# Spreading softmax probabilities as 32-bit words, a changed load order and program order, in a one-core decode block

## The chip, the cores and the metric

The kernel runs on one core of a Trainium2 chip. The metric is the time of one execution in device microseconds (us). In a trace, time counts from the start of the core's span; the span of the kernel before was 86.6 us where its time was 88.59, so some 2 us lie outside it. PE is the matrix engine (PEld its weight loads), DVE the vector engine, ACT the scalar engine, POOL is GpSimd, and SP issues the loads. PSUM is the memory that PE's results stand in, and a load lands when its data has arrived. In the views, `[1.76 <-issue]` means that the engine idled 1.76 us before this line and that the profile shows nothing that it waited for; another name after the arrow is what it waited for. The granted clock is a share of PE's full clock. L123 is a line of the kernel, with numbers of its own in each version.

## The reference

One decode step of a block with conditioned layer norms: four sequences, one new token each, width 512, 32 query heads on 8 key/value heads of 128, the last 1024 of 4096 cached positions, a feed-forward layer of 1792.

```python
mod = (silu(c) @ w_mod).reshape(4, 6, 1, 512)            # sa, ca, ga, sb, cb, gb
h = layernorm(x) * (1 + ca) + sa
q = (h @ wq) ...                                         # 32 heads x 128
scores = q @ k[:, :, -1024:].T * Dh ** -0.5              # per sequence and head
o = softmax(scores) @ v[:, :, -1024:]
x = x + ga * (o @ wo)
h = layernorm(x) * (1 + cb) + sb
x = x + gb * (relu(h @ w1) @ w2)
```

The arithmetic is small. What is large is what has to be read: K and V windows, w_mod, wq, wo, w1 and w2, about 32 MB.

## The kernel before

All large loads go through one queue, in this order: w_mod, three K tiles, wq, five K tiles, eight V tiles, wo in four quarters, w1, and w2 in three pieces. A tile of K or V is 1 MB. The 11 buffers for K and V and the shared buffers of w_mod with w1/w2 and of wq with wo make late loads wait for early readers; the trace shows 1.7 us of that, in four pieces, all of them V loads waiting for K tiles to be transposed.

```python
    KAHEAD = 3
    ...
    nc.sync.dma_start(out=wmod_sb[:], in_=w_mod...)
    for gi in range(KAHEAD): load_k(gi)
    for t in range(DT): nc.sync.dma_start(out=wq_sb[:, t, :], in_=wq_src[:, t, :])
    for gi in range(KAHEAD, NG): load_k(gi)
    ...                                                   # V, wo, w1
    W2_CHUNKS = [(0, 3), (3, 6), (6, FT2)]
    for (m0, m1) in W2_CHUNKS:
        nc.sync.dma_start(out=w2_dst[:, m0:m1, :], in_=w2_src[:, m0:m1, :])
```

The scores of all heads and sequences stand in one 128 x 1024 PSUM tile. For P times V (P: the probabilities) they have to be transposed, and each row must be spread over four column slots, of which only that of its own sequence may be nonzero. The kernel does this per quarter of the columns, with a 0/1 mask `m4`. Three slots are written by DVE, the fourth by GpSimd:

```python
    for iq in range(NQ):                                  # four quarters of 256
        nc.scalar.activation(out=e_sb[:, ws], in_=sc_ps[:, ws], func=ACT.Exp, ...)   # fp32
        for b in range(B):
            eng = nc.gpsimd if b == B - 1 else nc.vector
            eng.tensor_scalar_mul(out=p_rep[:, ws, b], in0=e_sb[:, ws], scalar1=m4[:, b:b + 1])
        ...                                               # 8 transposes into PSUM, copy to pT
```

The order of the instructions on each engine is chosen by the framework's scheduler. After P times V (`oT_ps`) come the output projection (`y_ps`, fed by wo), the second layer norm, and the feed-forward products (`u_ps` with w1, `z_ps` with w2).

Of the kernel before, what the change touches and what calls it, by code (L numbers as in the profile page):

```python
# [8 lines left out]
ACT = mybir.ActivationFunctionType  # L9
ALU = mybir.AluOpType  # L10
AX = mybir.AxisListType
bf16 = mybir.dt.bfloat16
f32 = mybir.dt.float32


@with_exitstack
def kernel(
# [14 lines left out]
    nc = tc.nc  # L32
    P = 128
# [19 lines left out]
    RB = KC  # L53
    KAHEAD = 3

    const = ctx.enter_context(tc.tile_pool(name="const", bufs=1))
    wts = ctx.enter_context(tc.tile_pool(name="wts", bufs=1))
    kvpool = ctx.enter_context(tc.tile_pool(name="kvpool", bufs=11))
    ktp = ctx.enter_context(tc.tile_pool(name="ktp", bufs=KAHEAD + 1))
    work = ctx.enter_context(tc.tile_pool(name="work", bufs=1))  # L60
# [7 lines left out]

    wmod_sb = wts.tile([P, DT, 6 * D], bf16, tag="med", name="wmod_sb")
    nc.sync.dma_start(out=wmod_sb[:], in_=w_mod.rearrange("(t p) n -> p t n", p=P))  # L70

# [3 lines left out]
    def load_k(gi):  # L75
        b, par = gi // 2, gi % 2
        kt_ = kvpool.tile([P, NI, Dh], bf16, tag="kv", name=f"k{gi}")
        nc.sync.dma_start(
            out=kt_[:].rearrange("p j d -> p (j d)"),
            in_=k_src[b, par, :, S - W:, :].rearrange("h (p j) d -> p h (j d)", j=NI),  # L80
        )
        k_tiles.append(kt_)

    for gi in range(KAHEAD):
        load_k(gi)
    wq_sb = wts.tile([P, DT, Hq * Dh], bf16, tag="big", name="wq_sb")
    wq_src = A_wq.rearrange("(t p) n -> p t n", p=P)
# [31 lines left out]
    for (m0, m1) in W2_CHUNKS:  # L119
# [4 lines left out]
    ident_bf = const.tile([P, P], bf16, name="ident_bf")  # L124
    make_identity(nc, ident_bf[:])
    ident_f = const.tile([P, P], f32, name="ident_f")
    make_identity(nc, ident_f[:])
# [5 lines left out]
    nc.gpsimd.memset(eps_t[:], EPS)  # L133
    siluT32 = const.tile([P, DT, CG], bf16, name="siluT32")
    nc.gpsimd.memset(siluT32[:], 0.0)

    ident_k = const.tile([P, P], bf16, name="ident_k")
    nc.vector.tensor_copy(out=ident_k[:].rearrange("p (h k) -> p h k", h=NHW),
                          in_=ident_bf[:].rearrange("p (k h) -> p h k", h=NHW))

    sel_l = const.tile([P, NL, P // NL], bf16, name="sel_l")
    nc.vector.tensor_copy(out=sel_l[:], in_=ident_bf[:].rearrange("p (k l) -> p l k", l=NL))

    m4 = const.tile([P, B], f32, name="m4")
    nc.vector.tensor_reduce(out=m4[:], in_=ident_f[:].rearrange("p (hp b r) -> p b hp r", b=B, r=rep),
                            axis=AX.XY, op=ALU.add)
    qpad = const.tile([P, B, 2, NHW, CG], bf16, name="qpad")
    nc.gpsimd.memset(qpad[:], 0.0)
    uT32 = const.tile([P, FT, CG], bf16, name="uT32")
    nc.gpsimd.memset(uT32[:], 0.0)  # L150
    NH = 2
    DH2 = D // NH
    xs2 = const.tile([P, DT, CG], f32, name="xs2")
# [18 lines left out]
    xT = work.tile([P, DT, B], f32, name="xT")  # L172
    nc.vector.tensor_copy(out=xT[:], in_=tp0[:, :, B:2 * B])


# [49 lines left out]

    sc_ps = psS.tile([P, W], f32, tag="s", name="sc_ps")
    IQ = NI // 4

    def k_transposes(gi):
        kT = ktp.tile([P, NI, NHW, KC], bf16, tag="kT", name=f"kT{gi}")  # L230
        for iq in range(4):
            tp = psA.tile([P, IQ, P], bf16, tag="t", name=f"ktp_{gi}_{iq}")
            for ii in range(IQ):
                nc.tensor.transpose(out=tp[:, ii, :], in_=k_tiles[gi][:, iq * IQ + ii, :], identity=ident_k[:])  # L234
            dst = kT[:, iq * IQ:(iq + 1) * IQ].rearrange("p i h k -> p i (h k)")
            if iq % 2 == 0:
                nc.vector.tensor_copy(out=dst, in_=tp[:])  # L237
            else:
                nc.scalar.copy(out=dst, in_=tp[:])  # L239
        return kT  # L240

    def k_scores(gi, kT):
        b, par = gi // 2, gi % 2
        for half in range(2):
            for hw in range(NHW):
                nc.tensor.matmul(  # L246
                    out=sc_ps[hw * CG:(hw + 1) * CG, half * HALF:(half + 1) * HALF],
                    lhsT=qpad[:, b, par, hw, :],
                    rhs=kT[:, half * (NI // 2):(half + 1) * (NI // 2), hw, :],
                    start=(gi == 0), stop=(gi == NG - 1),  # L250
                    tile_position=(0, hw * CG),
                )

    kts_pending = [k_transposes(gi) for gi in range(KAHEAD)]


    qT_ps = psA.tile([P, 2, NHW, rep, B], f32, tag="t", name="qT_ps")
    qT_v = qT_ps[:].rearrange("p a h r b -> p (a h r) b")
    for t in range(DT):
        for hq in range(Hq):  # L260
            nc.tensor.matmul(out=qT_v[:, hq, :], lhsT=wq_sb[:, t, hq * Dh:(hq + 1) * Dh], rhs=hT[:, t, :],  # L261
                             start=(t == 0 and hq == 0), stop=(t == DT - 1 and hq == Hq - 1))
    for gi in range(NG):
        b, par = gi // 2, gi % 2
        c0 = 16 * par + 4 * b
        src = qT_ps[:, par, :, :, b]
        if gi % 2 == 0:
            nc.vector.tensor_copy(out=qpad[:, b, par, :, c0:c0 + rep], in_=src)
        else:
            nc.scalar.copy(out=qpad[:, b, par, :, c0:c0 + rep], in_=src)  # L270

    for gi in range(KAHEAD - 1):
        k_scores(gi, kts_pending.pop(0))
    for gi in range(KAHEAD - 1, NG):
        if gi + 1 < NG:
            kts_pending.append(k_transposes(gi + 1))
        k_scores(gi, kts_pending.pop(0))


# [6 lines left out]
    IQ = NI // NQ  # L286
    e_sb = work.tile([P, W], f32, name="e_sb")
    den4 = work.tile([P, NQ], f32, name="den4")
    p_rep = ktp.tile([P, W, B], bf16, tag="kT", name="p_rep")
    pT = ktp.tile([P, NI, P], bf16, tag="kT", name="pT")  # L290
# [3 lines left out]
    def pv(h, i0, i1, first=False, last=False):  # L294
        par, hw = h // NHW, h % NHW
        c0 = 32 * hw + 16 * par
        for i in range(i0, i1):
            nc.tensor.matmul(out=oT_ps[:, hw, par].rearrange("p b r -> p (b r)"), lhsT=v_tiles[h][:, i, :],  # L298
                             rhs=pT[:, i, c0:c0 + B * rep], start=(first and i == i0), stop=(last and i == i1 - 1))

    VEARLY = 3
    for iq in range(NQ):
        ws = slice(iq * WQ, (iq + 1) * WQ)
        nc.scalar.activation(out=e_sb[:, ws], in_=sc_ps[:, ws], func=ACT.Exp, bias=nb[:], scale=scale,  # L304
                             accum_out=den4[:, iq:iq + 1])
        for b in range(B):
            eng = nc.gpsimd if b == B - 1 else nc.vector
            eng.tensor_scalar_mul(out=p_rep[:, ws, b], in0=e_sb[:, ws], scalar1=m4[:, b:b + 1])  # L308
        tp = psA.tile([P, IQ, P], bf16, tag="t", name=f"pT_ps{iq}")
        for ii in range(IQ):  # L310
            i = iq * IQ + ii
            nc.tensor.transpose(out=tp[:, ii, :], in_=p_rep[:, i * KC:(i + 1) * KC, :].rearrange("q k b -> q (k b)"),  # L312
                                identity=ident_bf[:])
        if iq % 2 == 0:
            nc.scalar.copy(out=pT[:, iq * IQ:(iq + 1) * IQ, :], in_=tp[:])  # L315
        else:
            nc.vector.tensor_copy(out=pT[:, iq * IQ:(iq + 1) * IQ, :], in_=tp[:])
# [9 lines left out]
    for iq in range(NQ):  # L327
        for h in range(VEARLY):
            pv(h, iq * IQ, (iq + 1) * IQ, first=(iq == 0 and h == 0))
    rb_ps = psA.tile([P, P], f32, tag="t", name="rb_ps")  # L330
    nc.tensor.matmul(out=rb_ps[:], lhsT=ones_f[:], rhs=rdiag[:], start=True, stop=True)
    rb = work.tile([P, P], f32, name="rb")
    nc.scalar.copy(out=rb[:], in_=rb_ps[:])
    for h in range(VEARLY, Hkv):
        pv(h, 0, NI, last=(h == Hkv - 1))
    oT_sb = work.tile([P, NHW, 2, B, rep], bf16, name="oT_sb")
    nc.vector.tensor_tensor(out=oT_sb[:].rearrange("p h a b r -> p (h a b r)"),
# [3 lines left out]
    for l in range(NL):  # L341
        for r in range(rep):
            nc.tensor.matmul(out=o4_ps[r * RB:(r + 1) * RB, l], lhsT=sel_l[:, l, :], rhs=oT_sb[:, :, :, :, r],
                             start=True, stop=True, tile_position=(0, r * RB))
# [20 lines left out]
    for t in range(DT):  # L365
        nh, tl = t // 2, t % 2
        nc.tensor.matmul(out=x12_ps[nh * CG:(nh + 1) * CG, tl * P:(tl + 1) * P], lhsT=xs2[:, t, :], rhs=ident_f[:],
                         start=True, stop=True, tile_position=(0, nh * CG))

    w1_cols = [w1_sb[:, t, :].rearrange("p (m2 q e) -> p m2 e q", q=P, e=2) for t in range(DT)]  # L370
# [60 lines left out]
```

## Time and profile before

| | before |
|---|---|
| time, median | 88.61 us (88.54 to 88.84, 3 runs) |
| span of the traced run | 86.6 us |
| read from HBM | 31.99 MB |
| PE / DVE / ACT / POOL busy | 63 / 32 / 27 / 11 % |

The slices, the chain of waits, the landings and the windows of the end are in the prediction below. Two more views belong to the argument. The groups of instructions that write the spread probabilities (busy us, mean ns of one, then idle time before them and what ended it):

```profile
L308 POOL TENSOR_SCALAR p_rep<-e_sb,m 128x256 bf16<-128x256 f32 x4 | 6.9, 1846 | 46.3 <-ACT e_sb L304 46.3
L312 PE MATMUL pT_ps<-ident_bf,p_rep 128*128 128x128 bf16 x32 | 4.1, 310 | 7.0 <-POOL p_rep L308 5.8
...
L308 DVE TENSOR_SCALAR p_rep<-e_sb,m 128x256 bf16<-128x256 f32 x12 | 4.4, 536 | 0.7 <-ACT e_sb L304 0.7
```

PE waits 5.8 us here for GpSimd's multiplies. And the timeline of PE near the end (start, length, instruction, idle before it):

```profile
68.99 0.41 PE L353 MATMUL y_ps<-o,wo_sb 128*128 128x4 bf16 x10 [0.40 <-DVE o L346]
71.16 3.29 PE L353 MATMUL y_ps<-o,wo_sb 128*128 128x4 bf16 x118 [1.76 <-issue]
...
80.13 3.17 PE L385 MATMUL z_ps<-w,uT 128*32 128x256 bf16 x28
```

### The profile page before, as it was taken

The numbers are of one execution on the slowest core, as the hardware profiler recorded it, in microseconds if no ns is written. First come the engines' busy times: TensorE is split into PE (matmuls) and PEld (weight loads), VectorE is DVE, ScalarE is ACT, GpSimd is POOL, SyncE is SP. The second block draws the span as 40 slices with busy tenths as digits, with TensorE's granted clock in tenths as the row PEclk, the third lists the DMA queues.
The fourth block names the chain that finished last, engine by engine and source line by source line (L and its number), as shares of the span: only waits on it lengthen the run. The fifth ranks groups of instructions, "written<-read, shape, count | busy, mean of one in ns | idle before, by whom it ended". The sixth has DMA issues, their size and how long they took to land.

```text
span 86.6 us, 2393 instructions
## 1 busy us (share of the span) xinstructions
PE 54.6 (63%) x1074; PEld 46.0 (53%) x1074; DVE 27.9 (32%) x74; ACT 23.4 (27%) x39; POOL 9.9 (11%) x19
## 2 busy tenths in 40 slices
PE   0000089799974389999997003959939619677940
PEld 0000086799974335778873003649939619557710
DVE  3704003373810030665453693283000200233130
ACT  2301001246950030877777260440100000020000
POOL 7600000000000000000000099920000000000000
PEclk9999999999998555999999985555555555555555
DMA  3799999999999999999999999999999999998100
GB/s 39 289 425 431 435 420 424 416 420 424 420 424 408 416 424 420 412 424 424 424 420 412 420 416 424 424 416 412 410 401 408 410 399 403 400 386 309 47 0 2
DMA packets 6009, 32.14 MB, mean 371 GB/s; under 512 B 480, under 2 KB 496, under 8 KB 3440
## 3 DMA queue, kind: packets, MB, share of 16 engines
q1 hardware_dynamic: 5976, 31.99, 91.0%
q8 instruction: 8, 0.13, 0.6%
q10 hardware_dynamic: 24, 0.01, 0.1%
q14 instruction: 1, 0.01, 0.0%
HBM read 31.99 MB, written 0.00 MB: 369 GB/s over the span
## 4 chain that ended last, share of the span: by engine, by line
PE 39%; DMA 33%; DVE 8%; issue 6%; ACT 5%; POOL 4%; POOLq 1%; DVEq 0%; ACTq 0%
DMA wq_sb<-in_A_wq_dram 21%; DMA wmod_sb<-in_w_mod_dram 12%; PE ktp L234 9%; PE oT_ps L298 8%; PE sc_ps L246 6%; PE y_ps L353 4%; POOL p_rep L308 4%; PE z_ps L385 4%; ACT kT L239 3%; PE pT_ps L312 2%; PE u_ps L378 2%; DVE p_rep L308 1%; DVE mx L281 1%; POOLq L426 1%; PE qT_ps L261 1%
## 5 line engine op out<-in xcount | busy, mean ns | idle before, releaser
L234 PEld LDWEIGHTS <-k 128*128 128x128 bf16 x256 | 17.0, 109 | 1.7 <-issue 1.7
L234 PE MATMUL ktp<-ident_k,k 128*128 128x128 bf16 x256 | 17.8, 238 | 0.0
L239 ACT COPY kT<-ktp 128x1024 bf16<-128x1024 bf16 x16 | 15.4, 1018 | 7.3 <-PE ktp L234 6.6
L237 DVE COPY kT<-ktp 128x1024 bf16<-128x1024 bf16 x16 | 11.1, 691 | 10.3 <-PE ktp L234 10.1
L308 POOL TENSOR_SCALAR p_rep<-e_sb,m 128x256 bf16<-128x256 f32 x4 | 6.9, 1846 | 46.3 <-ACT e_sb L304 46.3
L312 PE MATMUL pT_ps<-ident_bf,p_rep 128*128 128x128 bf16 x32 | 4.1, 310 | 7.0 <-POOL p_rep L308 5.8
L298 PE MATMUL oT_ps<-pT,v 128*128 128x16 bf16 x256 | 7.4, 175 | 1.4 <-issue 1.4
L298 PEld LDWEIGHTS <-v 128*128 128x128 bf16 x256 | 7.4, 105 | 1.6 <-issue 1.5
L312 PEld LDWEIGHTS <-p_rep 128*128 128x128 bf16 x32 | 3.1, 140 | 8.1 <-POOL p_rep L308 8.1
L246 PE MATMUL sc_ps<-kT,qpad 128*32 128x512 bf16 x64 | 6.5, 478 | 1.1 <-ACT kT L239 0.7
L261 PE MATMUL qT_ps<-hT,wq_sb 128*128 128x4 bf16 x128 | 3.9, 166 | 3.1 <-DMA wq_sb<-in_A_wq_dram 3.0
L261 PEld LDWEIGHTS <-wq_sb 128*128 128x128 bf16 x128 | 3.6, 99 | 3.4 <-DMA wq_sb<-in_A_wq_dram 3.4
L181 PE MATMUL mT<-siluT,wmod_sb 128*128 128x4 bf16 x80 | 2.3, 167 | 4.5 <-DMA wmod_sb<-in_w_mod_dram 4.5
L214 ACT ACTIVATE lnv_ln<-var_ln,eps_t 128x4 f32<-128x4 f32 x2 | 0.6, 298 | 16.7 <-DVE var_ln L212 16.7
L353 PE MATMUL y_ps<-o,wo_sb 128*128 128x4 bf16 x128 | 3.7, 166 | 2.2 <-issue 1.8
L353 PEld LDWEIGHTS <-wo_sb 128*128 128x128 bf16 x128 | 3.6, 104 | 2.2 <-issue 2.2
L181 PEld LDWEIGHTS <-wmod_sb 128*128 128x128 bf16 x80 | 2.2, 104 | 4.6 <-DMA wmod_sb<-in_w_mod_dram 4.6
L308 DVE TENSOR_SCALAR p_rep<-e_sb,m 128x256 bf16<-128x256 f32 x12 | 4.4, 536 | 0.7 <-ACT e_sb L304 0.7
L159 PE MATMUL tp<-ident_bf,cx_sb 8*128 8x8 bf16 x4 | 0.2, 163 | 6.4 <-DMA cx_sb<-in_A_x_dram 6.4
L246 PEld LDWEIGHTS <-qpad 128*32 128x32 bf16 x64 | 2.0, 109 | 3.8 <-issue 2.4
L159 PEld LDWEIGHTS <-cx_sb 8*128 8x128 bf16 x4 | 0.2, 100 | 6.4 <-issue 6.4
L315 ACT COPY pT<-pT_ps 128x1024 bf16<-128x1024 bf16 x2 | 2.0, 1012 | 4.6 <-PE pT_ps L312 4.6
(77 smaller groups left out, 42.7 us busy)
## 6 DMA issues: line engine op xcount, KB each, us to landing
k<-in_A_k_cache_dram SPq DMA_DIRECT2D x8, 1024.0 KB, 19.9
v<-in_A_v_cache_dram SPq DMA_DIRECT2D x8, 1024.0 KB, 20.2
wq_sb<-in_A_wq_dram SPq DMA_DIRECT2D x4, 1024.0 KB, 18.6
wo_sb<-in_A_wo_dram SPq DMA_DIRECT2D x4, 1024.0 KB, 20.1
wmod_sb<-in_w_mod_dram SPq DMA_DIRECT2D x1, 3072.0 KB, 10.4
w<-in_B_w_dram SPq DMA_DIRECT2D x1, 1792.0 KB, 22.2
w<-in_B_w_dram SPq DMA_DIRECT2D x2, 768.0 KB, 18.1
w<-in_B_w_dram SPq DMA_DIRECT2D x1, 256.0 KB, 13.7
```

What stands on the lines that cost most here:

```text
L181: nc.tensor.matmul(out=mT[:, k, m, :], lhsT=wmod_sb[:, t, n0:n0 + P], rhs=siluT32[:, t, 0:B], start=(t == 0), stop=(t == DT - 1))
L234: nc.tensor.transpose(out=tp[:, ii, :], in_=k_tiles[gi][:, iq * IQ + ii, :], identity=ident_k[:])
L237: nc.vector.tensor_copy(out=dst, in_=tp[:])
L239: nc.scalar.copy(out=dst, in_=tp[:])
L246: nc.tensor.matmul(out=sc_ps[hw * CG:(hw + 1) * CG, half * HALF:(half + 1) * HALF], lhsT=qpad[:, b, par, hw, :], rhs=kT[:, half * (NI // 2 ...
L261: nc.tensor.matmul(out=qT_v[:, hq, :], lhsT=wq_sb[:, t, hq * Dh:(hq + 1) * Dh], rhs=hT[:, t, :], start=(t == 0 and hq == 0), stop=(t == DT ...
L298: nc.tensor.matmul(out=oT_ps[:, hw, par].rearrange("p b r -> p (b r)"), lhsT=v_tiles[h][:, i, :], rhs=pT[:, i, c0:c0 + B * rep], start=(fi ...
L308: eng.tensor_scalar_mul(out=p_rep[:, ws, b], in0=e_sb[:, ws], scalar1=m4[:, b:b + 1])
L312: nc.tensor.transpose(out=tp[:, ii, :], in_=p_rep[:, i * KC:(i + 1) * KC, :].rearrange("q k b -> q (k b)"), identity=ident_bf[:])
L315: nc.scalar.copy(out=pT[:, iq * IQ:(iq + 1) * IQ, :], in_=tp[:])
L353: nc.tensor.matmul(out=y_ps[:, m, :], lhsT=wo_sb[:, h, l, m * P:(m + 1) * P], rhs=o4[:, l, h % NHW, h // NHW, :], start=(h == 0 and l == 0 ...
L385: nc.tensor.matmul(out=z_ps[nh * CG:(nh + 1) * CG, :], lhsT=uT32[:, m, :], rhs=w2_sb[:, m, nh * DH2:(nh + 1) * DH2], start=(m == 0), stop= ...
```

## The change

It takes GpSimd out of the softmax: exponentials are stored as bf16 in an order that puts two chunks' values into one 32-bit word, and DVE spreads such words with an AND against an all-ones or zero mask, four instructions in place of sixteen. It loads two K tiles before w_mod in place of three after it, and it runs PE, ACT, DVE and POOL in the order of the program text, with the softmax loop taken apart to suit. Some smaller things go with it: two copies of q in place of eight, a later broadcast of the denominator's reciprocal, constants in another order.

```diff
-    KAHEAD = 3
+    KAHEAD = 2
+    ctx.enter_context(tc.manual_schedule(engines={PE, Activation, DVE, Pool}))     # shortened
 ...
-    nc.sync.dma_start(out=wmod_sb[:], in_=w_mod...)
     for gi in range(KAHEAD):
         load_k(gi)
+    nc.sync.dma_start(out=wmod_sb[:], in_=w_mod...)
 ...
+    kts_pending = [k_transposes(gi) for gi in range(KAHEAD)]                       # now ahead of w_mod's matmuls
+    nc.vector.tensor_scalar_mul(out=mi4[:], in0=m4[:], scalar1=-1.0)               # int32: 0 or all ones
 ...
-    e_sb = work.tile([P, W], f32, name="e_sb")
+    e_sb = work.tile([P, W], bf16, name="e_sb")
+    e_w = e_sb[:].bitcast(i32)
-    p_rep = ktp.tile([P, W, B], bf16, tag="kT", name="p_rep")
+    p_rep = ktp.tile([P, NI // 2, P, 2], bf16, tag="kT", name="p_rep")
+    p_w = ...                                                                      # p_rep as 32-bit words
 ...
     for iq in range(NQ):
-        nc.scalar.activation(out=e_sb[:, ws], in_=sc_ps[:, ws], func=ACT.Exp, ...)
-        for b in range(B):
-            eng = nc.gpsimd if b == B - 1 else nc.vector
-            eng.tensor_scalar_mul(out=p_rep[:, ws, b], in0=e_sb[:, ws], scalar1=m4[:, b:b + 1])
+        nc.scalar.activation(out=e_sb[:, ws]..."q u k e", in_=sc_ps[:, ws]..."q u k e", func=ACT.Exp, ...)
+    for iq in range(NQ):
+        nc.vector.tensor_tensor(out=p_w[:, ws, :], in0=e_w[:, ws]..., in1=mi4[:]..., op=ALU.bitwise_and)
+    for iq in range(NQ):
         ...
-            nc.tensor.transpose(..., in_=p_rep[:, i * KC:(i + 1) * KC, :]...)
+            nc.tensor.transpose(..., in_=p_rep[:, i // 2, :, i % 2], ...)
```

More of the change, by code (lines that the diff above doesn't have):

```diff
@@ L13 @@
 f32 = mybir.dt.float32
+i32 = mybir.dt.int32
 @with_exitstack
@@ L53 @@
     RB = KC
-    KAHEAD = 3
+    KAHEAD = 2
+    NH = 2
+    DH2 = D // NH
+    ctx.enter_context(tc.manual_schedule(engines={
+        mybir.EngineType.PE, mybir.EngineType.Activation, mybir.EngineType.DVE, mybir.EngineType.Pool}))
     const = ctx.enter_context(tc.tile_pool(name="const", bufs=1))
@@ L58 @@
     kvpool = ctx.enter_context(tc.tile_pool(name="kvpool", bufs=11))
-    ktp = ctx.enter_context(tc.tile_pool(name="ktp", bufs=KAHEAD + 1))
+    ktp = ctx.enter_context(tc.tile_pool(name="ktp", bufs=4))
     work = ctx.enter_context(tc.tile_pool(name="work", bufs=1))
@@ L67 @@
     nc.scalar.dma_start(out=cx_sb[B:2 * B, :], in_=A_x.rearrange("b o d -> (b o) d"))
-    wmod_sb = wts.tile([P, DT, 6 * D], bf16, tag="med", name="wmod_sb")
-    nc.sync.dma_start(out=wmod_sb[:], in_=w_mod.rearrange("(t p) n -> p t n", p=P))
     k_src = A_k_cache.rearrange("b (par hw) s d -> b par hw s d", par=2)
@@ L85 @@
         load_k(gi)
+    wmod_sb = wts.tile([P, DT, 6 * D], bf16, tag="med", name="wmod_sb")
+    nc.sync.dma_start(out=wmod_sb[:], in_=w_mod.rearrange("(t p) n -> p t n", p=P))
     wq_sb = wts.tile([P, DT, Hq * Dh], bf16, tag="big", name="wq_sb")
@@ L125 @@
     make_identity(nc, ident_bf[:])
+    ident_k3 = const.tile([P, NHW, KC], bf16, name="ident_k")
+    nc.gpsimd.memset(ident_k3[:], 0.0)
+    nc.gpsimd.affine_select(out=ident_k3[:], in_=ident_k3[:], compare_op=ALU.not_equal, fill=1.0, base=0,
+                            pattern=[[-1, NHW], [-NHW, KC]], channel_multiplier=1)
+    ident_k = ident_k3[:].rearrange("p h k -> p (h k)")
+    siluT32 = const.tile([P, DT, CG], bf16, name="siluT32")
+    nc.gpsimd.memset(siluT32[:], 0.0)
     ident_f = const.tile([P, P], f32, name="ident_f")
@@ L133 @@
     nc.gpsimd.memset(eps_t[:], EPS)
-    siluT32 = const.tile([P, DT, CG], bf16, name="siluT32")
-    nc.gpsimd.memset(siluT32[:], 0.0)
-    ident_k = const.tile([P, P], bf16, name="ident_k")
-    nc.vector.tensor_copy(out=ident_k[:].rearrange("p (h k) -> p h k", h=NHW),
-                          in_=ident_bf[:].rearrange("p (k h) -> p h k", h=NHW))
-    sel_l = const.tile([P, NL, P // NL], bf16, name="sel_l")
-    nc.vector.tensor_copy(out=sel_l[:], in_=ident_bf[:].rearrange("p (k l) -> p l k", l=NL))
-    m4 = const.tile([P, B], f32, name="m4")
-    nc.vector.tensor_reduce(out=m4[:], in_=ident_f[:].rearrange("p (hp b r) -> p b hp r", b=B, r=rep),
-                            axis=AX.XY, op=ALU.add)
-    qpad = const.tile([P, B, 2, NHW, CG], bf16, name="qpad")
-    nc.gpsimd.memset(qpad[:], 0.0)
+    QB = 2 * NHW * CG
+    QS = QB + rep
+    qpad_f = const.tile([P, B * QS], bf16, name="qpad")
+    nc.gpsimd.memset(qpad_f[:], 0.0)
+    qpad = qpad_f[:, 0:B * QB].rearrange("p (b a h c) -> p b a h c", b=B, a=2, h=NHW)
+    qpad_s = qpad_f[:].rearrange("p (b x) -> p b x", b=B)
     uT32 = const.tile([P, FT, CG], bf16, name="uT32")
     nc.gpsimd.memset(uT32[:], 0.0)
-    NH = 2
-    DH2 = D // NH
     xs2 = const.tile([P, DT, CG], f32, name="xs2")
@@ L173, with k_transposes, k_scores @@
     nc.vector.tensor_copy(out=xT[:], in_=tp0[:, :, B:2 * B])
+    sc_ps = psS.tile([P, W], f32, tag="s", name="sc_ps")
+    IQ = NI // 4
+    def k_transposes(gi):
+        kT = ktp.tile([P, NI, NHW, KC], bf16, tag="kT", name=f"kT{gi}")
+        for iq in range(4):
+            tp = psA.tile([P, IQ, P], bf16, tag="t", name=f"ktp_{gi}_{iq}")
+            for ii in range(IQ):
+                nc.tensor.transpose(out=tp[:, ii, :], in_=k_tiles[gi][:, iq * IQ + ii, :], identity=ident_k)
+            dst = kT[:, iq * IQ:(iq + 1) * IQ].rearrange("p i h k -> p i (h k)")
+            if iq % 2 == 1:
+                nc.vector.tensor_copy(out=dst, in_=tp[:])
+            else:
+                nc.scalar.copy(out=dst, in_=tp[:])
+        return kT
+    def k_scores(gi, kT):
+        b, par = gi // 2, gi % 2
+        for half in range(2):
+            for hw in range(NHW):
+                nc.tensor.matmul(
+                    out=sc_ps[hw * CG:(hw + 1) * CG, half * HALF:(half + 1) * HALF],
+                    lhsT=qpad[:, b, par, hw, :],
+                    rhs=kT[:, half * (NI // 2):(half + 1) * (NI // 2), hw, :],
+                    start=(gi == 0), stop=(gi == NG - 1),
+                    tile_position=(0, hw * CG),
+                )
+    kts_pending = [k_transposes(gi) for gi in range(KAHEAD)]
+    m4 = const.tile([P, B], f32, name="m4")
+    nc.vector.tensor_reduce(out=m4[:], in_=ident_f[:].rearrange("p (hp b r) -> p b hp r", b=B, r=rep),
+                            axis=AX.XY, op=ALU.add)
+    mi4 = const.tile([P, B], i32, name="mi4")
+    nc.vector.tensor_scalar_mul(out=mi4[:], in0=m4[:], scalar1=-1.0)
     mT = psA.tile([P, 5, DT, B], f32, tag="t", name="mT")
@@ L223 @@
     layernorm_T(xT[:], g1[:], sa, hT[:], "ln1")
-    sc_ps = psS.tile([P, W], f32, tag="s", name="sc_ps")
-    IQ = NI // 4
-    def k_transposes(gi):
-        kT = ktp.tile([P, NI, NHW, KC], bf16, tag="kT", name=f"kT{gi}")
-        for iq in range(4):
-            tp = psA.tile([P, IQ, P], bf16, tag="t", name=f"ktp_{gi}_{iq}")
-            for ii in range(IQ):
-                nc.tensor.transpose(out=tp[:, ii, :], in_=k_tiles[gi][:, iq * IQ + ii, :], identity=ident_k[:])
-            dst = kT[:, iq * IQ:(iq + 1) * IQ].rearrange("p i h k -> p i (h k)")
-            if iq % 2 == 0:
-                nc.vector.tensor_copy(out=dst, in_=tp[:])
-            else:
-                nc.scalar.copy(out=dst, in_=tp[:])
-        return kT
-    def k_scores(gi, kT):
-        b, par = gi // 2, gi % 2
-        for half in range(2):
-            for hw in range(NHW):
-                nc.tensor.matmul(
-                    out=sc_ps[hw * CG:(hw + 1) * CG, half * HALF:(half + 1) * HALF],
-                    lhsT=qpad[:, b, par, hw, :],
-                    rhs=kT[:, half * (NI // 2):(half + 1) * (NI // 2), hw, :],
-                    start=(gi == 0), stop=(gi == NG - 1),
-                    tile_position=(0, hw * CG),
-                )
-    kts_pending = [k_transposes(gi) for gi in range(KAHEAD)]
     qT_ps = psA.tile([P, 2, NHW, rep, B], f32, tag="t", name="qT_ps")
@@ L262 @@
                              start=(t == 0 and hq == 0), stop=(t == DT - 1 and hq == Hq - 1))
-    for gi in range(NG):
-        b, par = gi // 2, gi % 2
-        c0 = 16 * par + 4 * b
-        src = qT_ps[:, par, :, :, b]
-        if gi % 2 == 0:
-            nc.vector.tensor_copy(out=qpad[:, b, par, :, c0:c0 + rep], in_=src)
-        else:
-            nc.scalar.copy(out=qpad[:, b, par, :, c0:c0 + rep], in_=src)
-    for gi in range(KAHEAD - 1):
+    for par in range(2):
+        dst = qpad_s[:, :, par * NHW * CG:(par + 1) * NHW * CG].rearrange("p b (h c) -> p b h c", h=NHW)
+        nc.vector.tensor_copy(
+            out=dst[:, :, :, 16 * par:16 * par + rep],
+            in_=qT_ps[:, par].rearrange("p h r b -> p b h r"))
+    for gi in range(KAHEAD):
         k_scores(gi, kts_pending.pop(0))
-    for gi in range(KAHEAD - 1, NG):
+    kts_pending.append(k_transposes(KAHEAD))
+    for gi in range(KAHEAD, NG):
         if gi + 1 < NG:
@@ L286 @@
     IQ = NI // NQ
-    e_sb = work.tile([P, W], f32, name="e_sb")
+    e_sb = work.tile([P, W], bf16, name="e_sb")
+    e_w = e_sb[:].bitcast(i32)
     den4 = work.tile([P, NQ], f32, name="den4")
-    p_rep = ktp.tile([P, W, B], bf16, tag="kT", name="p_rep")
+    p_rep = ktp.tile([P, NI // 2, P, 2], bf16, tag="kT", name="p_rep")
+    p_w = p_rep[:].rearrange("q u c e -> q (u c e)").bitcast(i32).rearrange("q (w b) -> q w b", b=B)
     pT = ktp.tile([P, NI, P], bf16, tag="kT", name="pT")
@@ L303 @@
         ws = slice(iq * WQ, (iq + 1) * WQ)
-        nc.scalar.activation(out=e_sb[:, ws], in_=sc_ps[:, ws], func=ACT.Exp, bias=nb[:], scale=scale,
-                             accum_out=den4[:, iq:iq + 1])
-        for b in range(B):
-            eng = nc.gpsimd if b == B - 1 else nc.vector
-            eng.tensor_scalar_mul(out=p_rep[:, ws, b], in0=e_sb[:, ws], scalar1=m4[:, b:b + 1])
+        nc.scalar.activation(out=e_sb[:, ws].rearrange("q (u k e) -> q u k e", k=KC, e=2),
+                             in_=sc_ps[:, ws].rearrange("q (u e k) -> q u k e", e=2, k=KC), func=ACT.Exp,
+                             bias=nb[:], scale=scale, accum_out=den4[:, iq:iq + 1])
+    for iq in range(NQ):
+        ws = slice(iq * WQ // 2, (iq + 1) * WQ // 2)
+        nc.vector.tensor_tensor(out=p_w[:, ws, :], in0=e_w[:, ws].unsqueeze(2).to_broadcast([P, WQ // 2, B]),
+                                in1=mi4[:].unsqueeze(1).to_broadcast([P, WQ // 2, B]), op=ALU.bitwise_and)
+    for iq in range(NQ):
         tp = psA.tile([P, IQ, P], bf16, tag="t", name=f"pT_ps{iq}")
@@ L311 @@
             i = iq * IQ + ii
-            nc.tensor.transpose(out=tp[:, ii, :], in_=p_rep[:, i * KC:(i + 1) * KC, :].rearrange("q k b -> q (k b)"),
-                                identity=ident_bf[:])
+            nc.tensor.transpose(out=tp[:, ii, :], in_=p_rep[:, i // 2, :, i % 2], identity=ident_bf[:])
         if iq % 2 == 0:
@@ L329 @@
             pv(h, iq * IQ, (iq + 1) * IQ, first=(iq == 0 and h == 0))
-    rb_ps = psA.tile([P, P], f32, tag="t", name="rb_ps")
-    nc.tensor.matmul(out=rb_ps[:], lhsT=ones_f[:], rhs=rdiag[:], start=True, stop=True)
-    rb = work.tile([P, P], f32, name="rb")
-    nc.scalar.copy(out=rb[:], in_=rb_ps[:])
     for h in range(VEARLY, Hkv):
         pv(h, 0, NI, last=(h == Hkv - 1))
+        if h == VEARLY:
+            rb_ps = psA.tile([P, P], f32, tag="t", name="rb_ps")
+            nc.tensor.matmul(out=rb_ps[:], lhsT=ones_f[:], rhs=rdiag[:], start=True, stop=True)
+            rb = work.tile([P, P], f32, name="rb")
+            nc.scalar.copy(out=rb[:], in_=rb_ps[:])
     oT_sb = work.tile([P, NHW, 2, B, rep], bf16, name="oT_sb")
@@ L342 @@
         for r in range(rep):
-            nc.tensor.matmul(out=o4_ps[r * RB:(r + 1) * RB, l], lhsT=sel_l[:, l, :], rhs=oT_sb[:, :, :, :, r],
+            nc.tensor.matmul(out=o4_ps[r * RB:(r + 1) * RB, l], lhsT=ident_k3[:, l, :], rhs=oT_sb[:, :, :, :, r],
                              start=True, stop=True, tile_position=(0, r * RB))
```

## The prediction

> **What bounds the kernel now.** I read the page's slices first, to see whether any resource is full for the whole span.
>
> ```profile
> DMA  3799999999999999999999999999999999998100
> GB/s 39 289 425 431 435 420 424 416 420 424 420 424 408 416 424 420 412 424 424 424 420 412 420 416 424 424 416 412 410 401 408 410 399 403 400 386 309 47 0 2
> ```
>
> One slice is 86.6 / 40 = 2.17 us. The reader is to see that the transfers are full from the third slice to the 36th and never dip, whatever the engines do. The page gives 31.99 MB read. TensorE, the busiest engine, is at 63%. So the kernel is a stream of about 32 MB, with compute hung on it. The chain of waits shows what hangs at the end of it:
>
> ```profile
> 49.88 3.55 POOL p_rep L308
> 53.43 1.13 POOLq L426
> 54.55 0.05 issue
> 54.60 1.05 PE pT_ps L312 x8
> ...
> 64.96 2.88 PE oT_ps L298 x102
> ...
> 71.16 3.30 PE y_ps L353 x118
> ...
> 78.57 1.63 PE u_ps L378 x56
> 80.20 3.12 PE z_ps L385 x28
> ```
>
> Columns: start, length, what. From 49.9 us to the end this is compute waiting for compute: GpSimd's quarter of the spreading of the probabilities, the transposes, P times V (oT_ps), the output projection (y_ps), the second layer norm, the two feed-forward products (u_ps, z_ps). The change shortens the beginning of this. What decides its worth is how far the chain runs behind the transfers that feed each stage. So I read the load queue: each transfer's issue time plus its time to landing (tile view of wo_sb, then the transfers of one window, where the second w2 load is issued).
>
> ```profile
> L109 SPq DMA_DIRECT2D wo_sb<-in_A_wo_dram x4: 368/376/385, 44.5 to 52.3; - x4
> DMA to landing us min/median/max: 20.1/20.1/20.1
> ```
>
> ```profile
> 64.23 3.63 SPq L120 DMA_DIRECT2D w<-in_B_w_dram  x1
> w<-in_B_w_dram SPq DMA_DIRECT2D x1, 768.0 KB, 16.8
> ```
>
> The last quarter of wo is issued at 52.3 and lands 20.1 us later, at 72.4. The second of the three w2 loads is issued at 64.23 and lands at 64.23 + 16.8 = 81.0. In the same way: the last V tile 42.1 + 20.2 = 62.3, w1 54.8 + 22.2 = 77.0, the first w2 load 59.5 + 19.5 = 79.0, the third 67.9 + 13.7 = 81.6. Finally the windows of the end (length, the engines' busy times, granted clock, DMA share, GB/s):
>
> ```profile
> 78.00:79.00 1.00, 0.50 (x19) 0.46 (x18) 0.35 (x3) 0.00 (x0) 0.00 (x0) 0.50 1.04 385
> 79.00:80.00 1.00, 1.00 (x44) 1.00 (x41) 0.18 (x1) 0.00 (x0) 0.00 (x0) 0.50 0.72 254
> 80.00:81.00 1.00, 1.00 (x18) 0.74 (x17) 0.35 (x2) 0.00 (x0) 0.00 (x0) 0.50 0.34 125
> ```
>
> [...] And z_ps, which needs the last weights, ends only at 83.3. The compute chain is **at most a microsecond or so behind the stream**, although it waited 6 us for GpSimd thirty microseconds earlier: the waits for V and wo already took most of that back.
>
> [...] The 28 z_ps matmuls, two beside each other in two column groups, took 3.12 us, so 223 ns a pair: the array is cold there (granted clock 0.50). [...]
>
> **The change, part by part.**
>
> 1. *Load order.* Two K tiles, then w_mod, then wq, in place of w_mod, three K tiles, wq. No byte is added or removed. One K tile (1.05 MB at 421 GB/s = 2.5 us) goes behind wq, so wq is complete at 29.6 - 2.5 = 27.1. From the fourth K tile on, the bytes ahead of every transfer are the same: K7 lands at 42.1 as before (the last V issue, which waits for it, starts then). The waits of the queue stay too: each load waits for the one eight before it, and the late V loads for K tiles to be transposed. That compute wait was 1.7 us in four pieces before, with some seven megabytes still queued, and it left no dip.
> 2. *Scores.* Transposing K0 and K1 fills PE's wait for w_mod, and two qpad copies replace eight alternating ones. From K3 on PE follows the transfers (1.89 + 0.66 = 2.55 us a tile against 2.5 us of landing). After K7's landing: 1.9 of transposes, 0.7 copy, 0.7 scores: 45.4 against 47.7.
> 3. *Softmax.* Out go the GpSimd multiplies (4 at 1.85 us, with their queue delays) and the 12 DVE multiplies (0.54 us each). In come four ANDs[...]. Max and its scaling 1.5 (47.0), the first exponential 0.5 (47.5),[...] the last eight transposes 1.05 and a copy 0.69: 52.0, against 58.86 + 0.69 = 59.55. This is **7.5 us of compute saved**. Reading p_rep with a step of two costs PE nothing much: u_ps reads its weights with that step already, at 1.63 us for 56 = 29 ns, against 3.30 / 118 = 28 ns for the unstrided y_ps.
> 4. *P times V.* 256 matmuls at about 28.6 ns (2.75 us for 96) are 7.3 us, so compute alone would end at 59.4. The last V tile lands at 62.3, plus its 32 x 28.6 = 0.9: 63.2, against 67.87. Of 7.5 us, 4.7 are left.
> 5. *Output projection.* The step between takes 68.99 - 67.87 = 1.1, so y_ps can start at 64.3. The last quarter of wo lands at 72.4, plus 32 x 28 ns = 0.9: 73.3 against 74.46. Left: 1.1.
> 6. *Feed forward.* From the end of y_ps to u_ps it takes 78.57 - 74.46 = 4.1: 77.4, with w1 there since 77.0. u_ps 1.6: 79.0. z_ps has 14 pairs at 0.223. The first six need the first w2 load (79.0): 80.4. Then it waits for the second (81.0), and eight pairs are left: 81.0 + 1.8 = 82.8, against 83.32. **Left: 0.5 us.** The gating of the result, its addition and the store follow as before.
>
> Sum: 88.61 - 0.5 = **88.1 us**, a change of 0.6%.
>
> **The rivals.**
>
> *The saving reaches the end.* If the stream were not the bound, the chain would end 5 to 7 us earlier, 81 to 83 us. For it speaks that the chain of waits names almost only compute after 50 us. Against it: the landing times, and full DMA slices throughout.
>
> *The stream itself ends earlier.* [...] If the new order[...] started the stream faster, all landings after 60 us could move forward by up to 1.5 us, and the time would be 86.3 to 87.2. [...] I see nothing in the change that touches it.
>
> *A warm array at the end.* PE's gap in the softmax falls from 5.8 us to about 3, so the clock may stay full for longer. [...] Against it: 9 us of nearly continuous P times V did not lift the clock from 0.50 before, and now PE waits for tiles more often.
>
> *Something new waits.* Program order could put a stalled instruction ahead of a ready one, or the AND or the strided exponential could be slower than estimated. Up to the output projection there are 8 us of slack (64.3 against 72.4), so twice the AND's time would still be hidden. Only a hold of the load queue would show: up to 89 us, and I see no such wait.
>
> **Range and chances.** The centre is the landing of the w2 loads plus fixed work. What can move it is the stream's end by a few tenths either way,[...] the clock downwards. Predicted 88.1 us, range 87.3 to 88.7. Faster by over 2% means below 86.84, which needs a second rival at nearly full size: 0.08. Slower by over 2% needs a stalled queue: 0.02. Within 2%: 0.90.
>
> **What would show it right or wrong.** Right: slices still full to the end, wo and w2 landing at the same times within 0.3 us, probabilities transposed by about 52 us, gaps in P times V and y_ps that end with landings, y_ps ending near 73.3, z_ps near 82.8. Wrong: w2 landing a microsecond or more earlier (the stream moved),[...] or y_ps ending after 74 (compute still bounds).

Passages are cut from this text, with the cuts marked. The softmax sum of part 3 came to 52.0 us with the four ANDs in it, whose length was the author's estimate (no trace had the operation then). So the 52.0, the 7.5 us saved and the 59.4 of part 4 stand as recorded, but cannot be added up from what is left. The sum at the end, 88.61 - 0.5 = 88.1 us, keeps all its terms, since it goes from landing to landing. The "up to 1.5 us" of the rival on the stream was the author's estimate, not shown, and the rival on the clock came to 87.2 us.

Three things that the prediction uses, as the trace of the kernel before shows them: the stream held 421 GB/s over 12 to 28 us and 418 over 52 to 60. The fifth V tile, issued at 34.61, lands 20.2 us later, at 54.8, and w1, eight loads behind it, is issued at 54.81. The granted clock was 1.00 from 36 to 51 us and 0.50 from 52 to 86, with PE idle from 47.7 to 53.5; that the idle time made it fall is not shown.

## The result

The changed kernel took **87.86 us** (median of 4 runs, 87.81 to 87.92), the kernel before 88.68 in the same comparison (88.54 to 88.84, 4 runs). The ratio is 0.991, with a 95% interval of 0.989 to 0.993: faster by about 0.8 us, within 2%. All runs were fast ones (a run counts as slow when it is over 1.5% above the fastest of its kernel). A ratio here is the mean time of one kernel's fast runs over that of the other's fast runs of the same rounds, so it is not quite the ratio of the medians quoted.

The slices of the changed kernel:

```profile
DMA  0799999999999999999999999999999999999200
GB/s 2 329 415 412 414 425 425 428 426 415 426 426 423 415 423 419 415 411 423 426 407 419 419 426 426 430 407 411 411 402 411 413 396 410 399 389 353 101 0 2
```

The stream is much as before: full from the third slice to the 37th (before: to the 36th), at about the same rates (417 to 426 GB/s over the 8 us windows between 12 and 60 us, before 417 to 421). The groups that spread the probabilities now:

```profile
L326 PE MATMUL pT_ps<-ident_bf,p_rep 128*128 128x128 bf16 x32 | 3.1, 278 | 2.9 <-DVE p_rep L320 2.9
...
L320 DVE TENSOR_TENSOR p_rep<-e_sb,mi 128x512 int32<-128x512 int32 x4 | 2.5, 688 | 0.7 <-ACT e_sb L315 0.7
```

An AND takes 0.69 us, and PE waits 2.9 us in place of 5.8. The timeline shows where that went (the row reduction behind the scores, the last copy of transposed probabilities, then PE):

```profile
46.60 1.23 DVE L290 TENSOR_REDUCE mx<-sc_ps 128x1 f32<-128x1024 f32 x1 [0.51 <-PE sc_ps L199]
...
52.63 0.69 DVE L330 COPY pT<-pT_ps 128x1024 bf16<-128x1024 bf16 x1 [0.82 <-PE pT_ps L326]
...
62.20 1.02 PE L309 MATMUL oT_ps<-pT,v 128*128 128x16 bf16 x32 [1.48 <-DMA v<-in_A_v_cache_dram]
...
69.83 1.01 PE L367 MATMUL y_ps<-o,wo_sb 128*128 128x4 bf16 x32 [1.52 <-DMA wo_sb<-in_A_wo_dram]
...
72.38 1.01 PE L367 MATMUL y_ps<-o,wo_sb 128*128 128x4 bf16 x32 [1.53 <-DMA wo_sb<-in_A_wo_dram]
...
79.07 1.47 PE L400 MATMUL z_ps<-w,uT 128*32 128x256 bf16 x12
80.82 1.89 PE L400 MATMUL z_ps<-w,uT 128*32 128x256 bf16 x16 [0.29 <-DMA w<-in_B_w_dram]
```

The last head of V, each quarter of wo and the second piece of w2 are now waited for. The transposed probabilities are ready at 53.3 us, against 59.5 before: 6.2 us saved. P times V ends at 63.2 (4.6 saved), y_ps at 73.4 (1.1 saved), z_ps at 82.7 (0.6 saved). Each wait for a transfer takes a part of the gain back. The landings themselves (tile view of wo_sb, then the issue and landing of the second w2 piece):

```profile
L114 SPq DMA_DIRECT2D wo_sb<-in_A_wo_dram x4: 368/376/387, 44.8 to 52.2; - x4
DMA to landing us min/median/max: 20.1/20.1/20.1
```

```profile
64.09 3.63 SPq L125 DMA_DIRECT2D w<-in_B_w_dram  x1
w<-in_B_w_dram SPq DMA_DIRECT2D x1, 768.0 KB, 16.7
```

The last quarter of wo lands at 52.2 + 20.1 = 72.3 (72.4 before), the second w2 piece at 64.09 + 16.7 = 80.8 (81.0 before). So the chain that ended last has turned from compute to transfers:

```profile
64.09 16.70 DMA w<-in_B_w_dram
...
80.82 1.90 PE z_ps L400 x16
...
82.75 0.43 DVE zg L410
```

And in the windows of the end the mean busy share of the DMA engines (the last figure but one) falls off over the same two microseconds as before. The view gives only this mean; when single engines finish is not shown:

```profile
79.00:80.00 1.00, 1.00 (x16) 0.74 (x14) 0.31 (x2) 0.00 (x0) 0.00 (x0) 0.50 0.62 234
80.00:81.00 1.00, 0.71 (x9) 0.33 (x7) 0.00 (x0) 0.00 (x0) 0.00 (x0) 0.50 0.39 139
```

### The profile page after: what moved, and what is told of

Its sections match the earlier page's. It is cut to its first block, busy times and chain, and to the rows that moved or that the text cites. A ratio compares the mean times of both kernels' runs of the same rounds, so it can differ in the third digit from the quotient of the medians.

```text
span 86.1 us, 2373 instructions
## 1 busy us (share of the span) xinstructions
PE 53.5 (62%) x1074; PEld 45.0 (52%) x1074; DVE 23.7 (28%) x63; ACT 22.8 (26%) x35; POOL 3.5 (4%) x17
## 4 chain that ended last, share of the span: by engine, by line
DMA 69%; SPq 15%; PE 10%; DVE 1%; issue 1%; DVEq 0%
DMA wq_sb<-in_A_wq_dram 27%; DMA v<-in_A_v_cache_dram 23%; DMA w<-in_B_w_dram 19%; SPq L119 5%; SPq L125 5%; PE ktp L187 5%; PE z_ps L400 2%; PE sc_ps L199 2%; SPq L94 2%; SPq L81 1%; PE qT_ps L271 1%; SPq L90 1%; DVE zg L410 0%; DVE res L412 0%; DVE qpad L275 0%
## 5 line engine op out<-in xcount | busy, mean ns | idle before, releaser
L199 PE MATMUL sc_ps<-kT,qpad 128*32 128x512 bf16 x64 | 5.6, 445 | 0.4 <-DVE qpad L275 0.4
L326 PE MATMUL pT_ps<-ident_bf,p_rep 128*128 128x128 bf16 x32 | 3.1, 278 | 2.9 <-DVE p_rep L320 2.9
L400 PE MATMUL z_ps<-w,uT 128*32 128x256 bf16 x28 | 3.4, 415 | 0.3 <-DMA w<-in_B_w_dram 0.3
L320 DVE TENSOR_TENSOR p_rep<-e_sb,mi 128x512 int32<-128x512 int32 x4 | 2.5, 688 | 0.7 <-ACT e_sb L315 0.7
L400 PEld LDWEIGHTS <-uT 128*32 128x32 bf16 x28 | 2.0, 137 | 1.1 <-issue 0.6
## 6 DMA issues: line engine op xcount, KB each, us to landing
wo_sb<-in_A_wo_dram SPq DMA_DIRECT2D x4, 1024.0 KB, 20.1
```

The costliest lines, as they stand in the source:

```text
L199: nc.tensor.matmul(out=sc_ps[hw * CG:(hw + 1) * CG, half * HALF:(half + 1) * HALF], lhsT=qpad[:, b, par, hw, :], rhs=kT[:, half * (NI // 2 ...
L326: nc.tensor.transpose(out=tp[:, ii, :], in_=p_rep[:, i // 2, :, i % 2], identity=ident_bf[:])
L400: nc.tensor.matmul(out=z_ps[nh * CG:(nh + 1) * CG, :], lhsT=uT32[:, m, :], rhs=w2_sb[:, m, nh * DH2:(nh + 1) * DH2], start=(m == 0), stop= ...
```

## The experiments

**Theory.** Before, compute from the softmax on was at most some tenths of a microsecond behind the transfers that feed the end. The change moves it ahead of them, and everything beyond that is lost in waits for V, wo and w2. **Rivals.** Compute still sets the end and the parts of the change add up; or it is one part, the AND or the program order, that brings the gain; or the stream moved. Twelve runs, all correct by the comparison with the reference, each timed beside the kernel before on its chip. Runs of one chip are compared with each other: e1 to e4 ran on a first chip (kernel before 89.13 us), e5 to e8 on a second (88.63), e9 to e12 on a third (88.76).

### The parts alone (e1 to e4)

**e1**: the kernel before with the AND alone.

```diff
 # in the kernel before
-    e_sb (f32), 16 multiplies by m4 per softmax, p_rep [P, W, B]
+    e_sb (bf16), 4 bitwise ANDs with mi4, p_rep [P, NI // 2, P, 2], loop in three parts   # as in the change
```

> The kernel before with the 32-bit AND in place of the multiplies, and nothing else of the change. Theory (the end is set by the landing of the second w2 load at about 81 us; compute before the output projection has slack): the chain starts as late as before (scores end at 47.7) but the softmax is some 7 us shorter, so y_ps follows the landings of wo, z_ps waits for the w2 load, and nearly the whole gain is there: 87.8 to 88.1 us, ratio 0.990 to 0.994. Rival (the parts add up, each giving its share of the 0.8 us): about 0.5 of 0.8 us, 88.2, and the rest in the other parts.

Measured: 87.87 us, ratio 0.988 (0.983 to 0.992). The gain of the whole change is there; the time itself, beside the changed kernel's 87.86, says so better than the ratio, since the kernel before is at the slow end of its scatter on this chip (see the feed-forward point below, in the part on why the prediction was right). Its timeline of PE waits like that of the changed kernel:

```profile
72.70 1.01 PE L360 MATMUL y_ps<-o,wo_sb 128*128 128x4 bf16 x32 [1.52 <-DMA wo_sb<-in_A_wo_dram]
...
81.21 1.89 PE L392 MATMUL z_ps<-w,uT 128*32 128x256 bf16 x16 [0.34 <-DMA w<-in_B_w_dram]
```

**e2**: the changed kernel with the old spreading put back.

```diff
 # in the changed kernel
-        nc.vector.tensor_tensor(out=p_w[:, ws, :], ..., op=ALU.bitwise_and)
+        for b in range(B):
+            eng = nc.gpsimd if b == B - 1 else nc.vector
+            eng.tensor_scalar_mul(out=p_rep[:, ws, b], in0=e_sb[:, ws], scalar1=m4[:, b:b + 1])
```

> The changed kernel with the old spreading put back (12 DVE and 4 GpSimd multiplies, fp32 exponentials). Theory: scores still end at 46.6, 1.1 us earlier than before, and that is just what y_ps was late by; P times V ends near 67, y_ps near 73.4 to 73.8, z_ps waits for w2 as in the changed kernel or misses it by a few tenths: 87.8 to 88.2 us, although 7 us of compute are back on the chain. Rival (the AND is the cause of the gain): the time goes back to that of the kernel before, 88.6.

Measured: 87.75 us, ratio 0.986 (0.982 to 0.990): no slower than with the AND. The multiplies cost their time again, but y_ps is complete at 70.13 + 3.34 = 73.5, against 73.4 in the changed kernel:

```profile
68.45 0.35 PE L365 MATMUL y_ps<-o,wo_sb 128*128 128x4 bf16 x8 [0.40 <-DVE o L358]
70.13 3.34 PE L365 MATMUL y_ps<-o,wo_sb 128*128 128x4 bf16 x120 [1.33 <-issue]
```

In the kernel before it is complete at 74.5. Some 0.4 of this 1.0 us come from a shorter gap without a shown wait (1.33 us in place of 1.76), the rest from the earlier scores. After that its z_ps waits for w2 (landing at 80.64), as in the changed kernel. So the AND alone suffices, and the rest without the AND suffices too. The parts do not add up.

**e3**: the kernel before with the load order of the change.

```diff
 # in the kernel before
-    KAHEAD = 3        # w_mod, 3 K tiles, wq, 5 K tiles
+    KAHEAD = 2        # 2 K tiles, w_mod, wq, 6 K tiles; scores loop to match
```

> The kernel before with only two K tiles loaded ahead of wmod and wq (the scores loop changed to go with it); the engines scheduled as before, multiplies kept. Theory: scores end about a microsecond earlier, which y_ps needs; 87.8 to 88.3 us. Rival (program order is what makes the earlier K tiles useful): no gain, 88.5 to 88.8.

Measured: 88.05 us, ratio 0.989 (0.985 to 0.993). One run of six was slow (91.52) and is left out of the ratio. By the time itself this too gives most of the gain (median of the fast runs 88.04): the scores end at 46.9 + 0.4 = 47.3 in place of 47.7, y_ps at 70.80 + 3.28 = 74.1 (74.5), z_ps at 82.9 (83.3). It does so without a wait for w2, so here compute still ends the program, by a little. One rival stays open: the fast runs of e3 have a mean granted clock of 0.80, those of the kernel before on this chip 0.745 to 0.781, and no run separates what the clock gives from what the load order gives.

**e4**: the kernel before in program order, nothing else.

```diff
 # in the kernel before
+    ctx.enter_context(tc.manual_schedule(engines={PE, Activation, DVE, Pool}))
```

> The kernel before with the four engines in program order and nothing else. Theory: it shortens nothing on the chain (GpSimd still spreads the last quarter at 1.85 us apiece), 88.5 to 88.8 us, ratio 1.00 within 0.3%. Rival (program order gives part of the gain by itself): 88.0 to 88.3.

Measured: 94.07 us, ratio 1.054 (1.048 to 1.060), one of six runs slow. Both expectations missed. The timeline of ACT shows why:

```profile
49.24 0.47 ACT L306 ACTIVATE e_sb<-sc_ps,nb 128x256 f32<-128x256 f32 x1 [2.00 <-DVE nb L285]
...
52.91 1.01 ACT L317 COPY pT<-pT_ps 128x1024 bf16<-128x1024 bf16 x1 [3.10 <-PE pT_ps L314]
53.82 0.48 ACT L306 ACTIVATE e_sb<-sc_ps,nb 128x256 f32<-128x256 f32 x1
...
60.31 1.01 ACT L317 COPY pT<-pT_ps 128x1024 bf16<-128x1024 bf16 x1 [5.46 <-PE pT_ps L314]
61.22 0.48 ACT L306 ACTIVATE e_sb<-sc_ps,nb 128x256 f32<-128x256 f32 x1
```

The old loop goes quarter by quarter. In program order the second exponential stands behind the copy of the first quarter's transposes, and the fourth behind that of the third. The scheduler of the kernel before had run all four exponentials ahead. The last one starts at 61.2 here, against 50.6 before.

**e10** settles it: e4 with the loop taken apart as the change has it.

```diff
 # in e4
             nc.scalar.activation(...)
+    for iq in range(NQ):
         for b in range(B): ...multiplies...
+    for iq in range(NQ):
         ...transposes and copies...
```

> The kernel before in program order as in e4 (94.1 us), but with the softmax loop taken apart as the change does it: all exponentials, then all multiplies, then all transposes and copies. Theory: e4's loss is ACT's second exponential standing behind the copy of the first quarter's transposed probabilities (49.6 to 53.8 us idle but for that copy), and so on for each quarter; taken apart, the order costs nothing: 88.3 to 88.9. Rival (program order loses elsewhere, in the K tiles or the layer norm): stays above 91.

Measured: 88.64 us, ratio 0.998 (0.992 to 1.004). Program order gives nothing by itself, and the three loops are what makes it harmless.

### Is the stream the bound, before and after (e5 to e7)

**e5 and e6**: the changed kernel and the kernel before, each without the load of the last V tile.

```diff
 # in both
-    for h in range(Hkv):
+    for h in range(Hkv - 1):
         ...load v_tiles[h]...
+    v_tiles.append(v_tiles[-1])        # head 7 reads head 6's V: wrong on purpose
```

> The changed kernel without the load of the last V tile (head 7 reads tile 6 again, so the result is wrong on purpose). All compute stays; the stream is 1.05 MB shorter, 2.5 us at 421 GB/s. Theory (the stream is the bound of the changed kernel): everything behind moves forward, 85.3 to 85.9 us, ratio about 0.965 to 0.97. Rival (a compute chain bounds it): no more than 0.5 us gained.

> The kernel before without the load of the last V tile (result wrong on purpose). Theory: there the compute chain from the softmax on ends the program, half a microsecond behind the landings, so a stream 2.5 us shorter gives little: 88.0 to 88.7 us. Rival (the stream bounded both): about 2.5 us gained, 86.2.

Measured: the changed kernel 85.23 us, ratio 0.962 (0.957 to 0.966); the kernel before 88.35, ratio 1.000 (0.993 to 1.006). (The comparison with the reference passed in both, so its tolerance does not see this error.) This is the clearest result. Take 2.5 us (1.05 MB at the 421 GB/s of the kernel before) out of the stream, and the changed kernel loses 2.6 (85.23 against the 87.78 of e7 on the same chip, which is as fast as the changed kernel), still waiting for w2; the kernel before loses nothing that its interval of 0.6% either way would show. Its y_ps runs as before:

```profile
68.77 0.41 PE L354 MATMUL y_ps<-o,wo_sb 128*128 128x4 bf16 x10 [0.40 <-DVE o L347]
...
70.93 3.28 PE L354 MATMUL y_ps<-o,wo_sb 128*128 128x4 bf16 x118 [1.76 <-issue]
```

```profile
78.37 1.89 PE L401 MATMUL z_ps<-w,uT 128*32 128x256 bf16 x16 [0.31 <-DMA w<-in_B_w_dram]
```

The first two lines are of e6, the last one of e5. The bound has moved from compute to the stream, although the time moved by 1% only.

**e7**: the changed kernel with each AND done twice.

```diff
         nc.vector.tensor_tensor(out=p_w[:, ws, :], ..., op=ALU.bitwise_and)
+        nc.vector.tensor_tensor(out=p_w[:, ws, :], ..., op=ALU.bitwise_and)     # the same again
```

> The changed kernel with each of the four ANDs done twice: 2.75 us more on DVE between the scores and P times V. Theory (slack there): y_ps still waits for each quarter of wo, time as the changed kernel's, 87.8 to 88.0. Rival (the softmax is on the path that sets the end): 90.5.

Measured: 87.78 us, ratio 0.991 (0.987 to 0.995), the changed kernel's time. Another 2.75 us in the softmax are hidden completely: y_ps still waits for the last quarter of wo, to 72.48, and z_ps ends at 82.75.

### Work behind the last landings (e8, e9, e11, e12)

The changed kernel still has eight pairs of z_ps to do when the second w2 piece lands, half of which need only its first part.

**e8 and e12**: that piece split.

```diff
 # in the changed kernel
-    W2_CHUNKS = [(0, 3), (3, 6), (6, FT2)]
+    W2_CHUNKS = [(0, 3), (3, 5), (5, 6), (6, FT2)]
```

> The changed kernel with the second w2 load (768 KB) split into 512 KB and 256 KB. Theory: z_ps waits for a load as a whole at 80.8 and has eight pairs of 0.22 us left then; with the split it starts four of them about 0.5 us earlier and only the last loads' two pairs each come behind their landing at about 80.9 and 81.5: z_ps ends near 82.0 in place of 82.7, 87.1 to 87.4 us. Rival ([...]the first part lands no earlier): 87.8.

> The changed kernel once more, on the chip of the other runs of this call: 87.8, for the comparison with e9 and e12.

> The kernel of e8 (second w2 load split) again with more rounds, beside the changed kernel on one chip: 0.3 to 0.5 us below it if the gain of e8 is real, equal if it was the chip.

Measured: e8 87.45 us, ratio 0.986 (0.981 to 0.991). Again with more rounds, on one chip: the changed kernel (e11) 87.83 (87.70 to 87.96, ratio 0.989), the split (e12) 87.34 (87.16 to 87.45, ratio 0.983 with 0.978 to 0.988). The two ranges do not touch: the split is faster by 0.5 us. In e8, z_ps runs in one piece again:

```profile
79.08 3.17 PE L400 MATMUL z_ps<-w,uT 128*32 128x256 bf16 x28
```

It ends at 82.25. The wait for w2 is gone, and PE's own time from the last quarter of wo on is the bound, so a finer split should give no more (no run tried one).

**e9**: the split, with dense matmuls in PE's waits, meant to lift the granted clock (0.50 in e8 from 78 to 82 us).

```diff
 # in e8's kernel
+    warm(3)      # after each of the first three quarters of y_ps: 3 matmuls of 512 columns, result unused
+    warm(1)      # after the last one, before the second statistics matmul of layer norm 2, and before u_ps
```

> The split w2 loads of e8, plus dense 512-column matmuls into an unused PSUM bank (three behind each of the first three quarters of y_ps, one in each gap of the second layer norm) so that PE is busy in the waits. With the split, z_ps takes 3.1 us at the cold clock without waiting for a load (79.15 to 82.27). Theory: if the fill lifts the clock, z_ps [...]ends right behind the last landing, near 81.8: 0.4 us less than the split alone, 87.0. Rival (the fill does not lift the clock through the layer norm and u_ps): as the split alone or up to half a microsecond slower.

How much less z_ps would take at a higher clock is cut from this expectation: it was the author's estimate, which no trace shows.

Measured: 87.25 us, ratio 0.982 (0.977 to 0.988), beside 87.34 for the split alone: the ranges overlap, so no gain is shown. z_ps still takes 3.17 us. The windows (after the length: PE busy, PEld, DVE, ACT, POOL, granted clock, DMA share, GB/s):

```profile
74.00:77.00 3.00, 2.65 (x14) 1.57 (x14) 1.03 (x6) 0.50 (x2) 0.00 (x0) 0.50 1.04 394
77.00:79.00 2.00, 2.00 (x59) 1.64 (x60) 0.71 (x5) 0.00 (x0) 0.00 (x0) 0.50 1.08 389
```

PE is shown busy for 4.65 of 5 us before z_ps, and the clock stays at 0.50. In the kernel before it was shown busy for 5.00 of 5 us from 58 to 63, and the clock was 0.50 there too; in the changed kernel, busy throughout from 50 to 56 us, the clock was 0.50 from 51 to 53 and 1.00 from 54 to 57. So this fill did not lift it, and what would is not shown.

## Why the prediction was right

The predicted time was 88.1 us in a range of 87.3 to 88.7, the measured one 87.86; the class, within 2%, was right too. Point by point:

- *Load order.* wq was predicted complete at 27.1; the last 32 matmuls that need it start at 27.40. No dip in the slices.
- *Scores.* They were predicted to end at 45.4 and ended at 46.5 (the maximum starts at 46.60). This term of the sum was mis-sized: I let PE follow K's landings, but it ran about 1.1 us behind them. The last K tile has landed by 42.3 (the last V load, which waits for it, is issued then), and its transposes start at 43.40. PE begins the third and fourth K tile at 30.63 at half clock (granted 0.50 over the window from 29 to 33 us, PE busy 4.00 of 4.00): their 64 transposes take 4.98 us, 32 later ones 1.96 (in the median 314 ns for one from 30.6 to 33 us, 219 from 36 us on, at a granted clock of 1.00 from 36 to 44). From then on it works through the tiles back to back at 2.44 us each (PE starts the last two at 40.96 and 43.40; it is busy 8.00 of 8.00 us from 36 to 44), about as fast as they land, and does not catch up. That the low clock made the delay is read from the trace; no run changed it.

```profile
30.63 4.98 PE L187 MATMUL ktp<-ident_k,k 128*128 128x128 bf16 x64
...
43.40 1.96 PE L187 MATMUL ktp<-ident_k,k 128*128 128x128 bf16 x32
```

- *Softmax.* An AND was measured at 688 ns; what the prediction took for it was an estimate. The stage saved 6.2 us in place of 7.5, nearly all of the difference being the late scores. e7 shows that this difference could not matter.
- *P times V.* Predicted 63.2, measured 63.2, ended by the last V tile.
- *Output projection.* Predicted 73.3, measured 73.4, ended by the last quarter of wo.
- *Feed forward.* Predicted: a wait for the second w2 piece at 81.0, z_ps to 82.8. Measured: a wait until 80.8, z_ps to 82.7. In the traces this gives 0.6 us in place of 0.5 (the store of the result is issued at 83.64, before at 84.23). The timed comparison gave 0.8. The kernel before scatters by over a microsecond, in groups that differ in the mean granted clock of the execution: of its 29 runs beside the experiments, the nine at 0.745 or 0.746 took 89.06 to 89.48 us, the eleven at 0.755 to 0.757 took 88.17 to 88.63 but for one of 89.08. (It is no simple slope: the other nine, at 0.759 to 0.783, took 88.58 to 89.44.) The ten runs of the changed kernel (0.695 to 0.723) stay within 87.70 to 87.96. So the gain is a mean over executions: about 0.5 us against the median of the eleven (88.35), 1.3 against that of the nine (89.20). What puts an execution into one group or the other was not tested, and with it the last 0.2 us stay open.
- *The rivals.* The saving did not reach the end. The stream did not end earlier by more than 0.2 us. The array was not warm at the end (granted clock 0.50). The rival "something new waits" was not true of the change, but e4 shows how near it was: program order with the old loop would have cost 5 us.
- *A wrong reading.* The prediction says that waits for V and wo had already taken back most of the 6 us lost to GpSimd. The trace of the kernel before has no such waits: PE's idle time before the matmuls on V (1.4 us) and most of that before those on wo (1.8 of 2.2) stand under "issue". None of the sums rests on it.

What the prediction did not see is that a part of the change is enough. It worked out the sum of all parts at each stage; the experiments show that the kernel before was so little behind the stream that the AND alone, or all but the AND, bring it there, and the load order alone nearly does.

One thing was taken as given and is only argued here. PE lost 1.43 us inside P times V and 1.76 us inside y_ps to "issue", each time while a 16 KB instruction packet was being fetched or had just arrived (packets from 62.4 and 68.6 us, of 1.0 us each). The second gap alone is more than y_ps was late by. In the changed kernel a gap of this kind (1.72 us, ending at 58.5) lies ahead of the wait for the last V tile, which takes it up. No run took these gaps away.

## What to carry to other kernels

Before valuing a saving in the middle of a kernel, add issue time and time to landing of every later load, and follow the saving from one such landing to the next: what is left at the last one is the gain, here 0.6 of 6.2 us. Removing one tile's load from both kernels, wrong result or not, tells at once which of them the stream bounds. Then look at what is left to do behind the last landings: splitting one 768 KB load in two gained 0.5 us beside the 0.8 of the whole change. And where engines run in program order, write each stage as a loop of its own: here that was worth over 5 us (e4 and e10).
